# Two-layer GELU network on one core: w1's first four tiles as two transfers behind the identity, and two dummy matmuls fewer

## The chip, the cores and the metric

The kernel runs on one core of a Trainium2 chip. The metric is the device time of the launch in microseconds (us). The kernel before was run eight times: median 94.19 us, from 94.01 to 94.66.

## The reference

```python
B, S, D, F = 1, 2048, 448, 1792          # all inputs bf16
h = jnp.einsum("bsd,df->bsf", x, w1) + b1
h = jax.nn.gelu(h, approximate=True)
return jnp.einsum("bsf,fd->bsd", h, w2) + b2
```

## The kernel before, in words

The 2048 rows of x are taken in four chunks of 512 (`SC`). For each chunk, layer 1 computes the hidden values transposed: F = 14 tiles of 128, two tiles at a time in one PSUM unit (`Layer1`, pairs j = 0 to 6). The contraction over D = 448 is three slabs of 128 (`k` = 0 to 2) and one of 64 (`k` = 3). Every slab of 128 is cut in two halves of 64 rows, so that two matmuls stand side by side on the two row halves of the array. `a()` is the first half of such a pair, `b()` the second, which also has the slab of 64; `act()` then has ScalarE evict the unit as GELU(h + b1) into `g`. Layer 2 multiplies `g` by w2, VectorE adds b2 on eviction, and SP stores. All of this is written as lists of operations, one for each engine (`Program.op`, `Program.dma`), and `emit` puts each list out in its own order with the semaphore waits of each operation in front of it. An `after=` is such a wait. So the order on an engine is the order of the calls below.

The start is what the change touches. Chunk 0 of x is loaded untransposed (`xn`, line 153, first on SP's queue), and TensorE transposes it: four tiles t with three 128x128 transposes each (`turn`, line 338), and two more for the last 64 columns (line 359). Each needs the identity, which GpSimd makes (lines 167 and 168). VectorE evicts tiles 0 and 2, ScalarE tiles 1 and 3 (`evac`, line 345), and both evict the last columns (line 368). The other chunks come transposed by DMA (line 147).

Ahead of the transposes TensorE runs seven dummy matmuls of 512 columns on a constant (`warm(NWARM)`, line 191), then one of 256 (`warm(1, HC)`), and behind the transposes another one of 256. Their result isn't used.

w1's first 384 rows are loaded in three transfers cut at tiles 0, 4, 8, 14 (`W1CUTS`, `load_w1`, line 130). The first, w1(0) with tiles 0 to 3, is on ScalarE's queue behind the activation that loads the GELU table (line 175); the others are on SP's queue, in this order behind a wait for that activation: w1r(0), w1(1), w1r(1), w1(2), w2 in two transfers, b2, and the transposed x. w1r is w1's last 64 rows (line 137). VectorE copies parts of it to the other row half (line 382), in its list behind four 32x32 transposes and a cast of b1 (lines 180 and 182). b1 itself comes by GpSimd's queue (line 173).

The matmuls of chunk 0 begin with pair 0 and pair 1 on the first 256 columns (12 matmuls; these need x's tiles 0 and 1 and w1's tiles 0 to 3), then both on the other 256 columns, then pair 0's second half with w1r, then pair 2's first half, which needs w1(1):

```python
for h in (0, HC):
    L[0].a(h, h + HC)
    L[1].a(h, h + HC)
L[0].b()
L[2].a()
L[1].b()
```

All layer-1 and layer-2 matmuls are recorded at line 216.

Of the kernel before, what the change touches and what calls it, by code (L numbers as in the profile page):

```python
# [73 lines left out]
def bass_standalone__dense_activation_gelu__prompt_kernel(  # L74
# [10 lines left out]
    P = 128  # L85
    H = P // 2
    SC = 512
    HC = SC // 2
# [5 lines left out]
    D3 = KT * P  # L94
# [3 lines left out]
    with ExitStack() as es:  # L98
# [3 lines left out]
        ident = sb("ident", [P, P], BF16)  # L102
        xT = sb("xT", [P, KT + 1, S], BF16)
        w1_sb = sb("w1_sb", [P, KT, F], BF16)
# [15 lines left out]
        ones_m = one.broadcast_to([P, SC])  # L120


        W1CUTS = (0, 4, 8, 14)

        def w1_of(ft):
            return max(i for i, c in enumerate(W1CUTS) if c <= ft)

        def load_w1(i, engine="sync"):
            c0, c1 = W1CUTS[i] * P, W1CUTS[i + 1] * P
            pr.dma(engine, lambda e: e.dma_start(  # L130
                w1_sb[:, :, c0:c1], w1[0:D3, c0:c1].rearrange("(k p) f -> p k f", p=P)), ("w1", i))

        RCUTS = (0, 4, 14)

        def load_w1r(i, engine="sync"):
            cs = slice(RCUTS[i] * P, RCUTS[i + 1] * P)
            pr.dma(engine, lambda e: e.dma_start(w1r[H:P, cs], w1[D3:D, cs]), ("w1r", i))

        def load_w2(a, b):
            pr.dma("sync", lambda e: e.dma_start(  # L140
                w2_sb[:, a:b, :], w2[a * P:b * P, :].rearrange("(f p) d -> p f d", p=P)), ("w2", a))
# [11 lines left out]
        pr.dma("sync", lambda e: e.dma_start(xn[:, :, :], x0v), "x")  # L153
        pr.barrier("sync", ["table"])
        load_w1r(0)
        load_w1(1)
        load_w1r(1)
        load_w1(2)
        load_w2(0, 7)
        load_w2(7, 14)  # L160
        pr.dma("sync", lambda e: e.dma_start(b2_bc[:, :], b2.partition_broadcast(P)), "b2")
        for c in range(1, NSC):
            for slot in range(KT + 1):
# [9 lines left out]
        pr.dma("gpsimd", lambda e: e.dma_start(b1n[0:NFT, :], b1.rearrange("(c p) -> c p", p=P)), "b1n",  # L173
               after=["b1z"])
        pr.op("scalar", lambda e: e.activation(junk[:, :], one, ACT.Gelu_apprx_tanh), event="table")  # L175
        load_w1(0, "scalar")

        def turn_b1():
            for q in range(4):
                pr.op("vector", lambda e, q=q: e.transpose(  # L180
                    b1t[32 * q:32 * q + 32, :], b1n[:, 32 * q:32 * q + 32]), after=["b1n"], event=("b1t", q))
            pr.op("vector", lambda e: e.tensor_copy(b1_f[:, :], b1t[:, 0:NFT]),
                  after=[("b1t", q) for q in range(4)], event="b1")
# [5 lines left out]
        def warm(n, cols=SC):  # L189
            for _ in range(n):  # L190
                pr.op("tensor", lambda e: e.matmul(unit[0][:, 0, 0:cols], lhsT=ones_w, rhs=ones_m[:, 0:cols],  # L191
                                                   start=True, stop=True))
# [156 lines left out]
        def turn_all():  # L349


            pr.op("vector", lambda e: e.tensor_copy(  # L352
                xr[:, :, :].rearrange("p q (two h) -> p q two h", two=2),
                xn[:, :, D3:D].rearrange("p (q two) h -> p q two h", two=2)), after=["x"], event="xr_in")
            for t in range(STC):
                turn(t)
                evac(("vector", "scalar")[t % 2], t)
            for q in range(STC // 2):
                pr.op("tensor", lambda e, q=q: e.transpose(  # L359
                    stage(0)[:, q * P:(q + 1) * P], xr[:, q, :], ident[:, :]),  # L360
                    after=["xr_in", ("xT0", 0)], event=("xr", q))
            halves = (slice(0, H), slice(H, P))
            for src, engine in enumerate(("vector", "scalar")):
                i = stage(0)[halves[src], 0:2 * P].rearrange("p (q s) -> p q s", q=2)
                for dst in (src, 1 - src):
                    o = xT[halves[dst], KT, 0:SC].rearrange("p (q two s) -> p q two s", q=2, two=2)[:, :, src, :]
                    pr.op(engine, lambda e, o=o, i=i, engine=engine:
                          e.copy(o, i) if engine == "scalar" else e.tensor_copy(o, i),  # L368
                          after=[("xr", 0), ("xr", 1)], event=("xR0", dst, src))
            busy[(3, 0)] = ("xR0", 1, 0)  # L370
            busy[(3, 2)] = ("xR0", 0, 1)

        warm(NWARM)
        warm(1, HC)
        turn_all()
        warm(1, HC)
        turn_b1()

        for i in (0, 1):
# [3 lines left out]
                  after=[("w1r", i)], event=("w1rU", i))  # L383
# [12 lines left out]
        for c in range(NSC):  # L396
# [7 lines left out]
            else:  # L404

                pr.op("vector", lambda e: e.tensor_copy(b2_z[H:H + 1, :], b2_bc[H:H + 1, :]),  # L406
                      after=["b2", "b2z0"], event="b2z")
# [3 lines left out]
            p = Layer2(c, (0, 1))  # L411
# [46 lines left out]
```

## Time and profile before

| | us |
|---|---|
| median of 8 runs (lowest, highest) | 94.19 (94.01, 94.66) |
| the profiled execution | 94.12 |
| its span, first to last instruction | 92.8 |
| TensorE matmul busy | 89.8 (97% of the span) |
| ScalarE busy | 38.5 |
| VectorE busy | 13.4 |
| GpSimd busy | 1.7 |

The span is 1.3 us shorter than the time of the same execution. Engines in the views are PE (TensorE matmuls), PEld (its weight loads), DVE (VectorE), ACT (ScalarE), POOL (GpSimd) and SP; a q behind the name is the engine's instruction queue, where DMAs are issued. In the timeline the columns are start, duration, engine, line, operation, output<-input, shape, count, and in brackets how long the engine had been idle and who ended that. In the list of DMAs the last columns are the number of transfers, the size of each and the median time from issue to landing.

### The profile page before, as it was taken

The numbers are of one execution on the slowest core, as the hardware profiler recorded it, in microseconds if no ns is written. First come the engines' busy times: TensorE is split into PE (matmuls) and PEld (weight loads), VectorE is DVE, ScalarE is ACT, GpSimd is POOL, SyncE is SP. The second block draws the span as 40 slices with busy tenths as digits, with TensorE's granted clock in tenths as the row PEclk, the third lists the DMA queues.
The fourth block names the chain that finished last, engine by engine and source line by source line (L and its number), as shares of the span: only waits on it lengthen the run. The fifth ranks groups of instructions, "written<-read, shape, count | busy, mean of one in ns | idle before, by whom it ended". The sixth has DMA issues, their size and how long they took to land.

```text
span 92.8 us, 2060 instructions
## 1 busy us (share of the span) xinstructions
PE 89.8 (97%) x932; PEld 63.1 (68%) x932; DVE 13.4 (14%) x33; ACT 38.5 (41%) x63; POOL 1.7 (2%) x8
## 2 busy tenths in 40 slices
PE   6999999999999999999999999999999999999990
PEld 2486777666667777666667777666667777687990
DVE  0183001010432000000433000000233000000421
ACT  6065888700004787800003787900002888900001
POOL 6000000000000000000000000000000000000000
PEclk9999999999999999999999999999999999999999
DMA  2999999554657100000032000000022000000022
GB/s 37 365 270 320 373 301 143 107 112 87 70 104 203 32 0 7 0 0 0 0 106 99 0 0 4 0 7 0 0 99 99 7 0 0 0 0 7 27 72 99
DMA packets 12344, 7.32 MB, mean 79 GB/s; under 512 B 6960, under 2 KB 12144, under 8 KB 12336
## 3 DMA queue, kind: packets, MB, share of 16 engines
q1 hardware_dynamic: 11904, 6.80, 31.5%
q10 hardware_dynamic: 400, 0.39, 1.2%
q8 instruction: 7, 0.11, 0.5%
q0 software_dynamic: 32, 0.00, 0.0%
q14 instruction: 1, 0.01, 0.0%
HBM read 3.79 MB, written 1.84 MB: 61 GB/s over the span
## 4 chain that ended last, share of the span: by engine, by line
PE 97%; ACT 0%; issue 0%
PE u L216 92%; PE u L191 4%; PE u L338 1%; ACT out_sb L328 0%; PE u L359 0%
## 5 line engine op out<-in xcount | busy, mean ns | idle before, releaser
L268 ACT ACTIVATE g<-u,b_f 128x512 bf16<-128x512 f32 x56 | 35.0, 685 | 39.8 <-PE u L216 39.8
L216 PE MATMUL u<-w_sb,g 64*128 64x448 bf16 (+1 forms) x504 | 43.7, 328 | 0.0
L216 PE MATMUL u<-xT,w_sb 64*128 64x512 bf16 (+1 forms) x348 | 42.7, 369 | 0.0
L216 PEld LDWEIGHTS u<-w_sb,g 64*128 64x128 bf16 x504 | 30.8, 94 | 12.1
L216 PEld LDWEIGHTS u<-xT,w_sb 64*128 64x128 bf16 x348 | 26.8, 94 | 10.1 <-issue 0.2
L311 DVE TENSOR_TENSOR out_sb<-u,b_bc 128x448 bf16<-128x448 f32 x14 | 8.1, 620 | 59.8 <-PE u L216 59.8
L216 PE MATMUL u<-xT,w1r 64*128 64x512 bf16 x56 | 14.9, 376 | 0.0
L216 PEld LDWEIGHTS u<-xT,w1r 64*128 64x128 bf16 x56 | 5.3, 94 | 2.1 <-DVE w1r L382 0.3
L191 PE MATMUL u<-const-bfloat16-1.0 128*128 128x512 bf16 (+1 forms) x9 | 3.6, 562 | 0.8 <-PEq L443 0.8
L328 ACT CAST out_sb<-u 128x224 bf16<-128x224 f32 x1 | 0.3, 347 | 9.3 <-PE u L216 9.3
L191 PEld LDWEIGHTS u<-const-bfloat16-1.0 128*128 128x128 bf16 x9 | 1.1, 132 | 2.4 <-issue 2.4
L345 ACT COPY xT<-u 128x384 bf16<-128x384 bf16 x2 | 0.9, 480 | 2.7 <-PE u L338 2.7
L175 ACT ACT_TABLE_LOAD x1 | 1.3, 1283 | 0.7 <-PEq L443 0.7
L338 PEld LDWEIGHTS u<-ident,xn 128*128 128x128 bf16 x12 | 1.1, 128 | 0.6 <-issue 0.6
L186 DVE COPY xT<-xT 64x512 bf16<-64x512 bf16 x3 | 0.9, 289 | 3.7 <-DMA xT<-in_x_dram 3.6
L406 DVE COPY b_z<-b_bc 1x448 bf16<-1x448 bf16 x1 | 0.3, 269 | 6.7 <-DMA b_bc<-in_b_dram 6.7
L338 PE MATMUL u<-ident,xn 128*128 128x128 bf16 x12 | 1.2, 274 | 0.0
L319 DVE TENSOR_TENSOR out_sb<-u,b_bc 128x448 bf16<-128x448 f32 x1 | 0.6, 625 | 1.8 <-PE u L216 1.8
L180 DVE STREAM_TRANSPOSE b1t<-b1n 32x32 bf16<-32x32 bf16 x4 | 0.8, 202 | 0.1
L345 DVE COPY xT<-u 128x384 bf16<-128x384 bf16 x2 | 0.7, 358 | 0.6 <-PE u L338 0.6
L368 ACT COPY xT<-u 64x256 bf16<-64x256 bf16 x2 | 0.7, 368 | 0.0
L352 DVE COPY xr<-xn 128x256 bf16<-128x256 bf16 x1 | 0.2, 227 | 3.0 <-DMA xn<-in_x_dram 3.0
(18 smaller groups left out, 4.8 us busy)
## 6 DMA issues: line engine op xcount, KB each, us to landing
out_dram<-out_sb SPq DMA_DIRECT2D x16, 112.0 KB, 1.7
w_sb<-in_w_dram SPq DMA_DIRECT2D x2, 784.0 KB, 8.6
w_sb<-in_w_dram SPq DMA_DIRECT2D x1, 576.0 KB, 6.3
xn<-in_x_dram SPq DMA_DIRECT2D x1, 448.0 KB, 3.2
w_sb<-in_w_dram ACTq DMA_DIRECT2D x1, 384.0 KB, 4.2
w_sb<-in_w_dram SPq DMA_DIRECT2D x1, 384.0 KB, 4.4
xT<-in_x_dram SPq DMA_TRANSPOSE x12, 4.3
w1r<-in_w_dram SPq DMA_DIRECT2D x1, 160.0 KB, 4.3
```

What stands on the lines that cost most here:

```text
L175: pr.op("scalar", lambda e: e.activation(junk[:, :], one, ACT.Gelu_apprx_tanh), event="table")
L180: pr.op("vector", lambda e, q=q: e.transpose(b1t[32 * q:32 * q + 32, :], b1n[:, 32 * q:32 * q + 32]), after=["b1n"], event=("b1t", q))
L186: pr.op("vector", lambda e: e.tensor_copy(xT[0:H, KT, s0:s1], xT[H:P, KT, s0:s1]), after=after, event=event)
L191: pr.op("tensor", lambda e: e.matmul(unit[0][:, 0, 0:cols], lhsT=ones_w, rhs=ones_m[:, 0:cols], start=True, stop=True))
L216: o = pr.op("tensor", lambda e: e.matmul(unit[u][:, lo, cols], lhsT=lhsT, rhs=rhs, start=start, stop=stop, skip_group_check=skip), after=a ...
L268: pr.op("scalar", lambda e, lo=lo, ft=ft: e.activation(g[:, ft, c * SC:(c + 1) * SC], unit[u][:, lo, :], ACT.Gelu_apprx_tanh, bias=b1_f[:, ...
L311: pr.op("vector", lambda e, lo=lo, j=j: e.tensor_tensor(out=out_sb[:, j, :], in0=unit[u][:, lo, 0:D], in1=b2_bc[:, :], op=ALU.add), after= ...
L319: pr.op("vector", lambda e: e.tensor_tensor(out=out_sb[:, j, :].rearrange("p (two h) -> p two h", two=2), in0=unit[u][:, :, 0:DH], in1=b2_ ...
L328: pr.op("scalar", lambda e: e.copy(out_sb[:, j, DH:D], unit[u][:, 1, 0:DH]), after=[y[1]], event=("o", j, 1))
L338: pr.op("tensor", lambda e, k=k: e.transpose(stage(t)[:, k * P:(k + 1) * P], xn[:, t, k * P:(k + 1) * P], ident[:, :]), after=["ident", "x ...
L345: pr.op(engine, lambda e: e.copy(o, i) if engine == "scalar" else e.tensor_copy(o, i), after=[("xt", t)], event=("xT0", t))
L368: e.copy(o, i) if engine == "scalar" else e.tensor_copy(o, i),
```

## The change

It cuts w1's first transfer in two, tiles 0 and 1 and tiles 2 and 3, both on ScalarE's queue, the first of them behind a wait for the identity. What was w1(1) and w1(2) on SP's queue is now w1(2) and w1(3), with the same tiles. The 256-column dummy ahead of the transposes and the one behind them are gone; the seven of 512 columns stay.

```diff
-        W1CUTS = (0, 4, 8, 14)
+        W1CUTS = (0, 2, 4, 8, 14)
...
-        def load_w1(i, engine="sync"):
+        def load_w1(i, engine="sync", after=()):
             c0, c1 = W1CUTS[i] * P, W1CUTS[i + 1] * P
             pr.dma(engine, lambda e: e.dma_start(
-                w1_sb[:, :, c0:c1], w1[0:D3, c0:c1].rearrange("(k p) f -> p k f", p=P)), ("w1", i))
+                w1_sb[:, :, c0:c1], w1[0:D3, c0:c1].rearrange("(k p) f -> p k f", p=P)), ("w1", i), after)
...
         load_w1r(0)
-        load_w1(1)
+        load_w1(2)
         load_w1r(1)
-        load_w1(2)
+        load_w1(3)
...
-        load_w1(0, "scalar")
+
+        load_w1(0, "scalar", ["ident"])
+        load_w1(1, "scalar")
...
         warm(NWARM)
-        warm(1, HC)
         turn_all()
-        warm(1, HC)
         turn_b1()
```

## The prediction

> **What bounds the kernel now.** I read the page's chain first, then the chain in order of time, then the start in the timeline, then the DMA list with its times to landing. Chain in order of time (start, length, what):
>
> ```profile
> 0.78 3.36 PE u L191 x8
> 4.14 1.14 PE u L338 x12
> 5.28 0.11 PE u L359 x2
> 5.39 0.11 PE u L191
> 5.50 0.04 issue
> 5.53 85.11 PE u L216 x906
> 90.64 0.02 issue
> 90.66 0.35 ACT out_sb L328
> ```
>
> From 5.53 us on TensorE works 85 us without a hole. The change touches none of that work; it can only move the moment when it starts, or open a hole in its first microseconds. So the question is what makes 5.53. The chain names the dummy of line 191, but that is only the instruction before. The timeline of the start:
>
> ```profile
> 0.74 0.39 SPq L153 DMA_DIRECT2D xn<-in_x_dram  x1
> 0.80 0.43 ACTq L130 DMA_DIRECT2D w_sb<-in_w_dram  x1
> 1.18 0.29 POOL L168 TENSOR_SCALAR_AFFINE_SELECT ident<-ident 128x128 bf16<-128x128 bf16 x1 [0.23 <-POOL ident L167]
> 2.27 0.55 SPq L137 DMA_DIRECT2D w1r<-in_w_dram  x1
> 2.87 0.57 SPq L130 DMA_DIRECT2D w_sb<-in_w_dram  x1
> 3.96 0.23 DVE L352 COPY xr<-xn 128x256 bf16<-128x256 bf16 x1 [3.04 <-DMA xn<-in_x_dram]
> 4.04 1.06 PEld L338 LDWEIGHTS u<-ident,xn 128*128 128x128 bf16 x12 [0.60 <-issue]
> 4.91 0.88 ACT L345 COPY xT<-u 128x384 bf16<-128x384 bf16 x2 [2.67 <-PE u L338]
> 5.22 0.27 PE L191 MATMUL u<-const-bfloat16-1.0 128*128 128x256 bf16 x1
> 5.50 0.14 PEld L216 LDWEIGHTS u<-xT,w_sb 64*128 64x128 bf16 x4 [0.23 <-issue]
> 7.37 0.22 DVE L382 COPY w1r<-w1r 64x256 bf16<-64x256 bf16 x1
> ```
>
> and of the DMA list:
>
> ```profile
> xn<-in_x_dram SPq DMA_DIRECT2D x1, 448.0 KB, 3.2
> w_sb<-in_w_dram ACTq DMA_DIRECT2D x1, 384.0 KB, 4.2
> w_sb<-in_w_dram SPq DMA_DIRECT2D x1, 384.0 KB, 4.4
> w1r<-in_w_dram SPq DMA_DIRECT2D x1, 64.0 KB, 3.4
> ```
>
> x lands at 0.74 + 3.2 = 3.94, and 0.1 later the transposes start (4.04). ScalarE evicts tile 1 from 4.91 on, 0.48 each, so to 5.39; 0.11 later the first real weight load stands at 5.50. w1(0) had landed at 0.80 + 4.2 = 5.0. So the start is x, transposes, ScalarE's eviction; w1(0) has some 0.4 us in hand.
>
> **First dummy.** The seven of 512 columns take 0.43 us each (their weight loads stand 0.43 apart), so they are issued out at 0.78 + 7 x 0.42 = 3.72. The eighth, half as wide, runs to about 3.94. That is just where x lands. Without it nothing starts sooner as long as x lands at 3.94: gain 0. It is worth something only if x comes sooner, up to 0.2 us; then it would have been the limit.
>
> **Second dummy.** It begins at 5.22 and holds the array for half of what a wide one takes: 0.21 us at the slow clock of the dummies, about 0.11 at the full one. In this execution it is done at 5.33 and the eviction releases the matmuls at 5.50: gain 0, cover 0.17. But the clock matters. The row of the transposes' weight loads reads
>
> ```profile
> L338 PEld LDWEIGHTS u<-ident,xn x12: 97/147/147, 4.0 to 5.0; 128*128 128x128 bf16 x12
> ```
>
> 147 ns at first and 97 at the last: the array runs slowly (dummies 0.43 apart; the page's clock row, full from the start, doesn't show this) and becomes fast at about 4.9. If it becomes fast later, the 14 transposes at 0.107 (9 start in the slow stretch 4.04 to 4.95) end their issue at 4.08 + 1.50 = 5.58 and the dummy at 5.79: then it holds up the matmuls by 0.21. The eight runs spread over 0.65 us, which the moment of the switch would explain (a microsecond of real matmuls at half clock costs 0.5). I take half the runs at 0.2: gain 0.1 in the median, bounds 0 and 0.21.
>
> **Transposes and the clock.** Here the Trainium skill speaks against the change ("TensorE: Matmul & The Clock Gate", Part 4: PE-mode transpose): in transpose mode the activity monitor doesn't count TensorE as busy, so the full clock doesn't engage. By that rule the two dummies are the only counted work between 3.7 and 5.5, and taking them away could cost a further window of slow clock, by Part 1 of that page 3.4 us, so half of it, 1.7 us. The row says otherwise: the clock rose inside the transposes, 0.9 us after the last dummy of the first group. And if uncounted transposes decided it, some of the eight runs should lie 1.7 us higher; the highest is 0.54 above the profiled one. I take 0 for this, with 1.7 as the bound at a small chance.
>
> **w1(0) issued later.** Today the issue starts at 0.80, 0.06 after x's, and x's first data competes with it at best in its set-up. In windows of the start the DMA engines move 172 GB/s from 2.0 to 2.5 us and 409 from 2.5 to 3.0. The slow first half microsecond costs x about 0.5 x (1 - 172/409) = 0.29 us. Whether ScalarE's transfer is the cause no view can say. If all of it goes, x lands 0.29 sooner; if none, 0; if the two new issues (1.5 and 1.95) disturb x midway, x could be 0.1 later. I take 0.1 sooner: the DMAs are different queues with one set of engines, and only part of the slow start need be theirs. With the first dummy gone, transposes, evictions and VectorE's chain (to line 382, which ends at 7.59 and for which a weight load waits today, 0.3 us in the waits) all follow x: the gain of 0.1 is not swallowed there.
>
> **The added wait.** The identity is done at 1.18 + 0.29 = 1.47. ScalarE's wait holds up nothing: its activation for the table is already in the engine (2.03), and its next work is at 4.91. Two issues of 0.43 end at 2.4. SP's queue waits for the activation, not for these.
>
> **When the two halves land.** w1(0), 393 KB, landed 1.1 us behind x. At that rate each half takes 0.55 us: 4.5 and 5.05. In the trace's packet records (not printed in a view) a packet of 256 bytes takes 18 ns, one of 1,024 bytes 46. The rows shrink from 1,024 to 512 bytes, by interpolation 27 ns, 48 rows for each DMA engine instead of 24: 1.30 us instead of 1.10, so 0.2 us more of DMA time (bounds 0 and 1.1, where a row costs the same at any length). First half 4.6, second 5.25. Needed: 5.4 for the first; for the second 5.53 + 6 matmuls of 0.055 = 5.86. Both are covered.
>
> **Who comes between.** SP's w1r(0) is issued at 2.27 and the next w1 at 2.87, against 1.95 for the second half. The Trainium skill ("DMA: Bandwidth & Descriptors", Queues, rings and completion order) says that each DMA engine takes turns between queues, a whole packet of descriptors at a time. By turns, the second half waits for w1r(0), 64 KB or 0.2 us, and lands at 5.45; if it had to let SP's 384 KB by as well, at 6.5, which is 0.65 late. The rows: a store of 112 KB needs 1.7 us to landing on idle queues, but w1r(0), 64 KB, took 3.4 and landed at 5.6, behind w1(0) at 5.0. So a transfer begun is drained first, and the order is about that of the issues. I take the first.
>
> **What the 0.2 us of DMA time does further on.** SP's next w1 lands at 2.87 + 4.4 = 7.3; pair 2 loads its first weights at 7.66. At 7.5 plus the 0.1 of a release it is just in time: cost 0, cover 0.06; if that is gone, up to 0.2. The last w1 transfer (10.3, needed at 10.7) stands alike.
>
> **Sum.** Profiled execution: 94.12 (span 92.8 and 1.3 around it) - 0.1 (x) - 0 (dummies, in its own clock phase) = 94.0. The median of the runs is 0.07 above it, and there the second dummy gives 0.1 more: 94.19 - 0.1 - 0.1 = 94.0.
>
> **The rivals.** *x gets the whole slow start back.* For it: 172 against 409 GB/s, and a first dummy that would have hidden just this. Against it: the rate may be low at the start of any load. 0.29 + 0.1: 93.8, down to 93.6. *Nothing moves.* x lands as before and the second dummy is covered: 94.15 to 94.25. *The second half, or SP's next w1, comes too late* (slower). Mechanism: ScalarE's second transfer falls behind SP's 384 KB; the price is (6.5 + 0.1) - 5.86 = 0.7 at pair 1's first matmul, less 0.2 of gain: 94.7. It decides from a landing of the second half later than 5.75, or of SP's w1 later than 7.55. For it: only 0.3 and 0.06 us in hand, and x itself took 1.0 us from issue to the first data (none move before 1.75). Against it: the issue is 0.9 us ahead of SP's. *The clock rises a window later* (slower): 95 to 95.7 in the runs that it hits.
>
> **How the numbers follow.** Small gain, 94.0 (93.75 to 94.25): 0.44. Large gain, 93.75: 0.17. Nothing: 0.10. Late weights, 94.7: 0.22. Clock: 0.07. A measurement of this kernel can tell about 0.3% (0.28 us). Faster by that (under 93.91): the large gain and under half of the small one, 0.35. Slower (over 94.47): most of late weights and clock, 0.27. Within: 0.38. The range from 93.6 to 94.7 leaves out the clock and half of late weights. The likeliest case alone: 93.75 to 94.25.
>
> **What would show it.** Right: x's copy on VectorE (line 352) at about 3.86 instead of 3.96, line 345 and the first weight load of line 216 sooner by as much, no wait of line 216 for a DMA, and weight loads of 97 ns by 5.5. Wrong: a wait on a w_sb transfer at 5.9 or 7.7 (late weights); weight loads of 147 ns behind 6 us (clock); line 352 at 3.96 (nothing gained at x).

## The result, and the profile after

The changed kernel takes 95.77 us (median of 11 runs, 94.86 to 97.75) against 94.28 (32 runs, 93.88 to 94.82): ratio 1.0123, interval 1.0093 to 1.0153. So it is slower, by about 1.2%; the prediction was 94.0, with a range up to 94.7. The ratio leaves out four executions of 97.2 to 97.8 us, in which the mean granted clock was 0.982 instead of 1.000; the median of 95.77 holds them, and without them it is 95.53.

The profiled execution took 95.26 us with a span of 93.9, 1.1 more than before. The chain in order of time (start, length, what):

```profile
0.74 1.18 ACT L175
1.92 0.03 issue
1.95 5.03 DMA w_sb<-in_w_dram
6.97 0.05 issue
7.02 84.75 PE u L218 x903
91.77 0.38 DVE out_sb L327
```

The chain no longer leads to TensorE's first matmuls but to a transfer of w1: issued at 1.95, that is ScalarE's second one, and landed at 6.97, 5.03 us later (line 218 is line 216 of before, moved by two). The timeline of the start shows the hole that it leaves:

```profile
1.50 0.96 ACTq L130 DMA_DIRECT2D w_sb<-in_w_dram  x2
2.87 0.57 SPq L130 DMA_DIRECT2D w_sb<-in_w_dram  x1
4.08 0.23 DVE L354 COPY xr<-xn 128x256 bf16<-128x256 bf16 x1 [3.15 <-DMA xn<-in_x_dram]
5.59 0.50 PE L218 MATMUL u<-xT,w_sb 64*128 64x256 bf16 x6
7.01 1.31 PEld L218 LDWEIGHTS u<-xT,w_sb 64*128 64x128 bf16 x24 [1.20 <-DMA w_sb<-in_w_dram]
7.02 1.80 PE L218 MATMUL u<-xT,w_sb 64*128 64x256 bf16 x24 [0.93 <-DMA w_sb<-in_w_dram]
```

Pair 0's six matmuls run at 5.59, on the first half of the weights, 0.06 later than before. The seventh matmul stood at 5.86 before and stands at 7.02 now. From there to the end of the matmuls both kernels take the same: 90.64 - 5.86 = 84.78 before, 84.75 after. So the 1.16 us by which the seventh matmul came later (0.06 of them from pair 0's later start, the rest from the wait) are the whole difference of the spans. x brought nothing: VectorE's copy, which shows x's landing, is at 4.08, not at the hoped 3.86. And while the second half was under way the DMA engines moved little (last column, GB/s; ahead of it the share of the time in which they were busy):

```profile
4.00:4.50 0.50, 0.31 (x4) 0.34 (x5) 0.23 (x1) 0.00 (x0) 0.00 (x0) 1.00 0.69 178
4.50:5.00 0.50, 0.50 (x10) 0.50 (x9) 0.29 (x1) 0.04 (x1) 0.00 (x0) 1.00 0.72 136
5.00:5.50 0.50, 0.48 (x7) 0.21 (x4) 0.42 (x2) 0.50 (x2) 0.00 (x0) 1.00 0.98 222
```

The kernel before in the same three windows:

```profile
4.00:4.50 0.50, 0.50 (x6) 0.46 (x6) 0.19 (x1) 0.00 (x0) 0.00 (x0) 1.00 1.10 374
4.50:5.00 0.50, 0.50 (x8) 0.50 (x6) 0.36 (x1) 0.09 (x1) 0.00 (x0) 1.00 0.89 201
5.00:5.50 0.50, 0.50 (x8) 0.27 (x5) 0.35 (x1) 0.50 (x2) 0.00 (x0) 1.00 0.94 317
```

It has such a dip too, but only when the data of its first w1 transfer are already through (its last packet ends at 4.53).

The packet records of the traces (printed in no view) show more of the late half. Each of these loads ends with sixteen packets of four bytes, apparently one for each of the 16 DMA engines. For w1(0) before, they lie between 4.28 and 4.52; for the second half after, between 4.48 and 6.60, eight of them by 5.54. So the landing tells of the last engine, and half of them were through a microsecond earlier. From 4.0 to 5.0 us ScalarE's queue has 227 packets of weights and SP's only 37, with the engines busy 0.7 of the time: SP's data aren't what slows the half in this microsecond. From 5.0 on, ScalarE's last 163 packets of 512 bytes stand among SP's, which are 311 of 1,024 bytes by 6.5.

### The profile page after: what moved, and what is told of

The parts are those of the page before. It is cut to its first block, busy times and chain, and to the rows that moved or that the text cites. A ratio compares the mean times of both kernels' runs of the same rounds, so it can differ in the third digit from the quotient of the medians.

```text
span 93.9 us, 2057 instructions
## 1 busy us (share of the span) xinstructions
PE 89.6 (95%) x930; PEld 46.0 (49%) x930; DVE 13.4 (14%) x33; ACT 38.4 (41%) x63; POOL 1.7 (2%) x8
## 4 chain that ended last, share of the span: by engine, by line
PE 90%; DMA 5%; ACT 1%; DVE 0%; issue 0%
PE u L218 90%; DMA w_sb<-in_w_dram 5%; ACT L175 1%; DVE out_sb L327 0%
## 5 line engine op out<-in xcount | busy, mean ns | idle before, releaser
L218 PE MATMUL u<-w_sb,g 64*128 64x448 bf16 (+1 forms) x504 | 43.2, 328 | 0.0
L218 PE MATMUL u<-xT,w_sb 64*128 64x512 bf16 (+1 forms) x348 | 41.0, 369 | 1.0 <-DMA w_sb<-in_w_dram 0.9
L218 PEld LDWEIGHTS u<-w_sb,g 64*128 64x128 bf16 x504 | 24.5, 94 | 18.4
L218 PEld LDWEIGHTS u<-xT,w_sb 64*128 64x128 bf16 x348 | 16.8, 94 | 20.4 <-DMA w_sb<-in_w_dram 1.2
L218 PE MATMUL u<-xT,w1r 64*128 64x512 bf16 x56 | 10.6, 376 | 0.0
L218 PEld LDWEIGHTS u<-xT,w1r 64*128 64x128 bf16 x56 | 2.7, 94 | 3.3
L193 PE MATMUL u<-const-bfloat16-1.0 128*128 128x512 bf16 x7 | 3.1, 624 | 0.8 <-PEq L443 0.8
L382 DVE COPY w1r<-w1r 64x256 bf16<-64x256 bf16 (+1 forms) x2 | 0.6, 288 | 1.4 <-DMA w1r<-in_w_dram 1.4
```

The costliest lines, as they stand in the source:

```text
L218: o = pr.op("tensor", lambda e: e.matmul(unit[u][:, lo, cols], lhsT=lhsT, rhs=rhs, start=start, stop=stop, skip_group_check=skip), after=a ...
L382: pr.op("vector", lambda e, odd=odd: e.tensor_copy(odd(slice(0, H)), odd(slice(H, P))), after=[("w1r", i)], event=("w1rU", i))
```

## The experiments

Theory after the result: the second half is late because it is issued 0.7 us later and so meets the transfers of SP's queue at the DMA engines (sharing). Rivals: the shorter rows and the further transfer are slow by themselves; the dummies' absence costs the time through the clock. Landings below are each from one profiled execution. How far they vary is seen in three kernels with the same loads (the changed kernel, `e2_w1_only` and `e7_filled_wait`): 6.97, 7.43 and 6.54. So a difference of less than 0.9 us between two single landings says little.

**Each part alone.** `e1_dummies_only`: the kernel before with this edit only.

```diff
         warm(NWARM)
-        warm(1, HC)
         turn_all()
-        warm(1, HC)
         turn_b1()
```

> The kernel before without its two 256-column dummies, w1 loaded as before. If the late second transfer is the whole cost (theory: sharing of the DMA engines), this run has no wait for w1 and takes 94.1 to 94.3, like before. If the dummies' absence costs the time through the clock (rival), it takes 95 or more, or some of its executions lie about 1.7 us higher with a mean granted clock near 0.98.

Ratio 1.0006, 0.9989 to 1.0022. The dummies' removal costs nothing and gains nothing that can be measured; the mean granted clock is 1.000 in all 22 executions.

`e2_w1_only`: the changed kernel with the two `warm(1, HC)` put back.

> The changed kernel with the two dummies put back: only the w1 loads are changed. Sharing theory: the wait at pair 1's first matmul stays, the second transfer lands near 7.0, 95.3 to 95.8. Clock rival: close to before, 94.2 to 94.5.

Ratio 1.0178, 1.0136 to 1.0221, mean clock 1.000 in all six executions; the second half lands at 7.43, 0.46 later than in the changed kernel's profile. The median, 96.04, is above the expected range; the interval of the ratio overlaps that of the changed kernel. The whole loss is in the w1 loads.

**The wait or the split.** `e3_no_wait`:

```diff
-        load_w1(0, "scalar", ["ident"])
+        load_w1(0, "scalar")
```

> The changed kernel without the wait for the identity: two transfers, issued from 0.8 on. Sharing theory: the second half is issued at about 1.25, data 0.7 us ahead of where it is in the changed kernel, begun before SP's w1 (issued at 2.87) has data; it lands by about 5.3 and no wait opens: 94.1 to 94.4. Rival (shorter rows and one more transfer are what is slow): the second half still lands after 6 and the time stays over 94.9.

The halves are issued at 0.80 and 1.26 and land 3.8 and 4.3 us later; no wait opens at pair 1. Median 94.60, above the expected range; ratio 1.0023, 1.0006 to 1.0041. The landing of the second half, 5.54, is 0.2 later than expected and 0.5 later than the one transfer of before (5.05); in the packet records its data end at 4.71 against 4.53. That is the split's own price as far as two single executions can tell, and it is hidden here up to 5.86. A part of what remains is one transfer later on: SP's last w1 lands at 10.97 instead of 10.36, and its first user waits 0.5 us.

`e4_one_transfer`: the delay without the split.

```diff
-        W1CUTS = (0, 2, 4, 8, 14)
+        W1CUTS = (0, 4, 8, 14)
...
         load_w1(0, "scalar", ["ident"])
-        load_w1(1, "scalar")
```

> The changed kernel with one transfer of four tiles on ScalarE's queue, behind the identity: the delay without the split. Sharing theory: the one transfer begins when x ends, as the first half does now (landing 4.6), but its second half's worth of rows meets SP's w1r(0) and w1 and shares with them: it lands between 5.3 and 6, and all 24 first matmuls wait for it: 94.4 to 95.0. Rival (rows and the number of transfers): it lands at 5.1 as before, 94.2.

Median 94.87, ratio 1.0050, 1.0025 to 1.0074. Issued 0.7 us later, the one transfer lands at 6.16, 1.1 later than before. So the delay alone costs time, without shorter rows and without a second transfer; that the landing moves by more than the delay is within the spread of single landings here. For the two halves it moves further: the second is issued 0.7 us later than in `e3_no_wait` and lands at 6.54 to 7.43 instead of 5.54. In time, the split alone costs 0.2%, the delay alone 0.5%, and both together 1.2%.

**Who is beside it.** `e5_sp_held`:

```diff
         load_w1r(0)
-        load_w1(2)
+        load_w1(2, after=[("w1", 1)])
```

> The changed kernel with SP's next w1 transfer (384 KB) and all behind it on SP's queue held until w1's second half has landed; only w1r(0), 64 KB, still runs beside it. Sharing theory: the second half lands by about 5.3 and pair 1 doesn't wait; SP's w1 is issued at 5.4 instead of 2.87 and lands near 8.0, so a wait of about 0.3 us opens at pair 2: 94.3 to 94.8. Rival (a transfer issued from 1.95 on ScalarE's queue is late by itself, by its issue or its short rows): the second half lands near 7.0 as before, and SP's w1 later still: over 96.

The second half lands at 5.94, a microsecond sooner than in the changed kernel, but not at 5.3. The second expectation failed clearly: SP's w1, issued at 5.96 on idle engines, landed 4.06 us later, at 10.02, and pair 2 waited 2.5 us instead of 0.3. Ratio 1.0224, 1.0176 to 1.0271; what it measures is mainly this second wait. It rests on two executions: in the other four, the profiled one among them, the mean clock was 0.982. In the profile the clock falls at 10.4 us, behind both landings.

`e6_one_queue`: both halves on SP's queue, ahead of w1r(0), just as late.

```diff
         pr.dma("sync", lambda e: e.dma_start(xn[:, :, :], x0v), "x")
+        load_w1(0, after=["ident"])
+        load_w1(1)
         pr.barrier("sync", ["table"])
...
-        load_w1(0, "scalar", ["ident"])
-        load_w1(1, "scalar")
```

> The changed kernel with both halves of w1's first four tiles on SP's queue, behind x and the same wait for the identity, ahead of w1r(0): issued at 1.5 and 2.05, as late as in the changed kernel, but in one queue with what follows. Sharing theory (turns are taken between queues, and one queue keeps its order): the halves land near 4.6 and 5.2, no wait at pair 1; SP's w1 is issued 0.35 later but its data queue anyway: 94.1 to 94.4. Rival (late issue or short rows): the second half lands after 6.5, 95 to 96.

The first half lands at 4.58, as expected, the second at 6.34, not 5.2: between the two theories, nearer to the second. Median 94.98, ratio 1.0052, 1.0026 to 1.0078. One queue in place of two isn't the cure, so turns between queues are at most a part.

`e7_filled_wait`: eight dummies in the wait.

```diff
             L[0].a(h, h + HC)
+            if h == 0:
+                for _ in range(8):
+                    pr.op("tensor", lambda e: e.matmul(unit[1][:, 0, 0:HC], lhsT=ones_w, rhs=ones_m[:, 0:HC],
+                                                       start=True, stop=True))
             L[1].a(h, h + HC)
```

> The changed kernel with eight 256-column dummies (on a PSUM unit that is cleared afterwards) between pair 0's first six matmuls and pair 1's, that is, inside the wait for w1's second half. If the wait alone is the cost, the dummies (0.86 us at full clock) lie within it: 95.0 to 95.8, as the changed kernel. If standing still for a microsecond also costs clock, the mean granted clock is 1.000 in all executions and the median falls below the changed kernel's 95.77.

Ratio 1.0150, 1.0104 to 1.0196. The second half came at 6.54 here and pair 1 began at 6.69, when the dummies were through. The mean clock is 1.000 in all six executions, but the median, 95.76, didn't fall: inconclusive for the time.

**Rows.** `e9_by_slab`: the first four tiles as one transfer of 128 rows and one of 256, all of 1,024 bytes.

```diff
-        load_w1(0, "scalar", ["ident"])
-        load_w1(1, "scalar")
+        for k0, k1, after in ((0, 1, ["ident"]), (1, KT, [])):
+            pr.dma("scalar", lambda e, k0=k0, k1=k1: e.dma_start(
+                w1_sb[:, k0:k1, 0:SC], w1[k0 * P:k1 * P, 0:SC].rearrange("(k p) f -> p k f", p=P)), ("w1k", k0), after)
```

> The changed kernel with the first four tiles cut by slabs of the contraction instead of by tiles: one transfer of 128 rows of 1,024 bytes and one of 256, behind the identity, both on ScalarE's queue; the number of rows and their length are those of the one transfer. Theory that the number of rows is the price (each row costs DMA time whatever its length, once the engines have used up what was queued): the last of the two lands as in the run with one delayed transfer, 5.5 to 6.2, and the time is 94.6 to 95.0. Theory that being a second transfer on ScalarE's queue beside SP's is the price: it lands near 7, 95.3 or more.

The last of the two lands at 6.41, 0.2 outside the first theory's window; median 95.10, ratio 1.0078, 1.0052 to 1.0104. It lies between the theories again. Half as many rows save about a third of the change's loss, with intervals that overlap; landings with a spread like the one above can't split it further.

`e10_probes`: the kernel before with loads into unused tiles in the middle of the kernel, each step behind the landing of the one before.

```diff
+                probe("sync", mz[0][:, :, :], cut(3, 256, 0), "pa", ["outA"])
+                probe("scalar", mz[1][:, :, :], cut(3, 256, 256), "pb", ["outA"])
+                probe("sync", mz[2][:, :, :], cut(3, 256, 0), "pc", ["pa", "pb"])
+                probe("sync", mz[3][:, :, :], cut(3, 256, 256), "pd", [])
+                probe("sync", mz[4][:, :, :], cut(3, 256, 512), "pe", ["pc", "pd"])
+                probe("sync", mw[:, :, :], cut(3, 512, 0), "pf", ["pe"])
+                probe("sync", ml[:, :], w2[0:D3, :].rearrange("(p t) d -> p (t d)", t=3), "pg", ["pf"])
+                probe("sync", ms[:, :], w1[0:P, 0:256], "ph", ["pg"])
```

> The kernel before with loads into unused tiles while the DMA engines are idle (behind chunk 0's stores); the outputs don't use them. First 384 rows of 512 bytes on SP's and on ScalarE's queue at once; then two such on SP's queue; then alone: 384 rows of 512, 384 rows of 1,024, 128 rows of 2,688, 128 rows of 512 bytes. If the number of rows is the price, 384 rows of 512 and of 1,024 bytes take nearly the same, about 3 to 4 us from issue to landing, and 128 long rows (344 KB) under 3. If turns between queues are the price, the pair on two queues takes over 1 us longer than the pair on one queue. If bytes are (what the prediction took), 384 rows of 512 bytes are 0.5 us quicker than those of 1,024, and both pairs are alike.

From its list of DMAs (size, us from issue to landing; ma and mb are the pair on two queues, mc and md the pair on one, the others alone):

```profile
mw_<-in_w_dram SPq DMA_DIRECT2D x1, 384.0 KB, 3.3
ml_<-in_w_dram SPq DMA_DIRECT2D x1, 336.0 KB, 2.9
ma_<-in_w_dram SPq DMA_DIRECT2D x1, 192.0 KB, 3.2
mb_<-in_w_dram ACTq DMA_DIRECT2D x1, 192.0 KB, 3.5
mc_<-in_w_dram SPq DMA_DIRECT2D x1, 192.0 KB, 2.7
md_<-in_w_dram SPq DMA_DIRECT2D x1, 192.0 KB, 2.8
me_<-in_w_dram SPq DMA_DIRECT2D x1, 192.0 KB, 3.1
ms_<-in_w_dram SPq DMA_DIRECT2D x1, 64.0 KB, 1.8
```

Alone, 384 rows of 512 bytes take 3.1 us and of 1,024 bytes 3.3: half the bytes save next to nothing. But a second such transfer right behind the first adds only 0.6 (the pair on one queue is issued at 33.78 and 34.21 and ends at 37.0), as the prediction's 27 ns a row has it (24 rows for each engine, 0.65). The pair on two queues ends 3.5 us after its issue, against 3.2 on one: turns cost 0.25 at most, and two transfers as alike as mc and me differ by 0.4. None of the three explanations gives 1.5 us by itself where nothing else is under way.

**How much company.** `e11_b1_on_sp` moves b1's transfer from GpSimd's queue to SP's, behind w1r(0).

> The changed kernel with b1's transfer (3.5 KB) moved from GpSimd's queue to SP's, behind w1r(0). If b1's packets from a third queue cause the slow stretch from 4.0 to 5.0 us, the second half lands by about 5.3 and the time is 94.2 to 94.5. If it is SP's w1 beside it, the second half still lands near 7, 95.3 to 95.8.

The second half lands at 6.85, so b1's queue isn't what makes it late. The median, 95.06, lies between the two expectations (ratio 1.0082, 1.0055 to 1.0108): about a third of the loss is gone, with intervals that overlap. If that is real, its cause isn't shown, since the move also puts SP's next w1 later (issued at 3.50 instead of 2.87). In this profile the first half was late, too: it landed at 5.76, and pair 0 waited 0.6 us for it. With the loads of the changed kernel it landed at 4.64, 4.55 and 5.03, so the prediction's cover for it (needed at 5.4) wasn't safe, either.

`e13_sp_one_ahead`:

```diff
         load_w1(2)
+        pr.barrier("sync", [("w1", 1)])
         load_w1r(1)
```

> The changed kernel with SP's w1r(0) and next w1 issued as now, but everything behind them on SP's queue held until w1's second half has landed. If SP's next w1 alone is the company that matters, the second half still lands at 6.5 to 7. If the further issues are (their descriptors), it lands near 5.9, as with all of SP held. Later transfers come late in both cases, so the time is over 95 and says little.

It lands at 6.69 (94.98 us, one execution), within the spread of the kernels with all of SP's transfers beside it: SP's next w1 is company enough.

`e14_alone`: the wait of SP's queue is for the second half, too, and b1 is on SP's queue behind w1r(0).

```diff
-        pr.barrier("sync", ["table"])
+        pr.barrier("sync", ["table", ("w1", 1)])
         load_w1r(0)
```

> The changed kernel with the two halves alone behind x: SP's queue, w1r(0) too, is held until the second half has landed, and b1 is on SP's queue behind that. If company is the cause, the halves land at 4.6 and 5.2, as the prediction worked out. If the start itself is slow (any second transfer behind x), the second half lands near 5.9 again. The time is over 96 in both cases, since all later weights are late.

The tile view of w_sb, for ScalarE's two transfers alone:

```profile
L130 ACTq DMA_DIRECT2D w_sb<-in_w_dram x2: 415/464/512, 1.5 to 1.9; - x2
DMA to landing us min/median/max: 3.4/3.5/3.5
```

They land at 4.90 and 5.45, and pair 1 waits for nothing. That is the 5.25 of the prediction within 0.2. (97.16 us, since all later weights come late.) In the packet records ScalarE's queue has 406 packets of weights from 4.0 to 5.0 us, instead of the changed kernel's 227, and the second half's four-byte packets lie between 4.50 and 5.16.

In the order of company the second half lands at 5.45 (none), 5.94 (w1r(0) and b1), 6.69 (SP's next w1 as well), 6.97 (all). Each is one execution; the first two lie clear of the 6.54 to 7.43 in full company, the third doesn't. The pieces of the chains (start, length) from which the landings of `e4_one_transfer`, `e5_sp_held`, `e6_one_queue` and `e13_sp_one_ahead` are read, in this order:

```profile
1.50 4.66 DMA w_sb<-in_w_dram
1.95 4.00 DMA w_sb<-in_w_dram
1.93 4.41 DMA w_sb<-in_w_dram
1.94 4.75 DMA w_sb<-in_w_dram
```

**A faster kernel?** `e8_w1r_first` is the kernel before without the two dummies and with VectorE's first copy of w1r ahead of b1's transposes:

```diff
-        turn_b1()
...
                   after=[("w1r", i)], event=("w1rU", i))
+            if i == 0:
+                turn_b1()
```

> An attempt at a faster kernel: the kernel before without the two dummies, with VectorE's first copy of w1r (line 382) ahead of b1's transposes and cast. In the profiles a weight load waits 0.3 to 0.4 us for that copy. The copy would end at about 6.35 instead of 7.6, b1 at 7.6, still ahead of the first GELU (7.9). One row half of the array gets its stall of 0.15 us back: 94.1 to 94.2 if it counts in full, 94.3 if the other row half sets the end.

Median 94.15 against 94.44 of the kernel before beside it, ratio 0.9983, 0.9963 to 1.0003: probably a little faster, not told apart from no change. `e12_w1r_first_b1_sp` is the same with b1 on SP's queue:

> The attempt at a faster kernel (kernel before without the two dummies, w1r's copy ahead of b1's transposes) with b1 on SP's queue behind w1r(0). If b1's queue causes the slow stretch, the other w1 transfers land sooner and nothing waits: 94.0. If not, as without the move, 94.15; b1 may land later than 5.3, but is needed only at 6.4.

Median 94.49, above both expectations; ratio 1.0021, 1.0005 to 1.0037: the move takes that away again. Here, too, SP's next w1 is issued at 3.50 instead of 2.87, and weight loads wait for w1 0.9 us in all.

## Why the prediction was wrong

- **Who comes between.** This is the step that failed. It took from w1r(0) and w1(0) that "a transfer begun is drained first, and the order is about that of the issues", and put the second half at 5.45. It landed at 6.97; without company at 5.45 (`e14_alone`), where the prediction had 5.25, so that the same figure twice is chance. Taking away SP's later transfers, SP's next w1, and w1r(0) with b1's queue gives back 0.3, 0.75 and 0.5, in one execution each. A single transfer issued 0.7 later lost 1.1 (`e4_one_transfer`). The row that I read as a rule showed a transfer 1.5 us ahead of the others, and the second half is 0.3 ahead of w1r(0) and 0.9 of SP's w1.
- **The rule that I set aside.** The Trainium skill ("DMA: Bandwidth & Descriptors", Queues, rings and completion order) has the engines take turns between queues. As the bound the prediction let SP's 384 KB by and got 6.5. That was nearer than my choice, and still short: the turns are at most 0.25 us where measured alone (`e10_probes`), and one queue for all brought 0.6 of 1.5 (`e6_one_queue`). What remains goes with the low rate between 4.0 and 5.5 us, 136 to 222 GB/s, in whose first microsecond SP's queue hardly moved data. The prediction worked with about 360 throughout (393 KB in 1.1 us) and made nothing of the window of 201 that the kernel before has at 4.5.
- **The slower rival.** Its place (pair 1's first matmul), its deciding point (5.75) and its mechanism (ScalarE's second transfer behind SP's 384 KB) were right but for one point: SP's 384 KB didn't go first. They landed at 8.4, and the two transfers went side by side. Its price was mis-sized: 0.7 less 0.2 of gain; measured 1.16 and no gain. Its chance, 0.22, came from the failed step.
- **x sooner.** Wrong. x takes 3.1 to 3.3 us to landing in every kernel here, with w1 issued at 0.8 or at 1.5, and the rate from 2.0 to 2.5 is no higher after the change (129 GB/s against 172). In the packet records SP's queue is the only one with data until 3.1 us, in the kernel before, too: no data of w1 stand beside x's slow start. What makes it slow stays open.
- **Dummies.** 0 for the first, as said; the 0.1 for the second isn't seen (1.0006, 0.9989 to 1.0022; 0.1 us would be the lower edge). By the Trainium skill ("TensorE: Matmul & The Clock Gate", Part 4: PE-mode transpose) TensorE doesn't count as busy in transpose mode and the full clock doesn't engage; the prediction set the 1.7 us that this could cost at nothing. That held: no execution of `e1_dummies_only` took more than 94.70 us, and in its profile the weight loads of the transposes take 95 to 98 ns, as at the full clock. Whether the transposes helped to raise it isn't shown, since the seven wide dummies stayed. The mean clock of 1.000 doesn't show it, because the kernel before has that mean, too, with a rise as late as 4.9.
- **The clock a window later.** No execution of the kernel before or of `e1_dummies_only` had it, but four of the changed kernel's twelve (with the profiled one) did. In the profiles of two such executions (`e11_b1_on_sp`, `e5_sp_held`) the granted clock is 0.50 for 3.4 us, from 6.9 and from 10.4, right behind waits for w1 of 0.6 and of 2.1 us. Half of 3.4 is 1.7; the four executions lie 1.7 to 2.2 above the 95.53 of the others. The prediction looked for this in the transposes, and not behind a hole.
- **The added wait** holds up nothing on ScalarE, as said, but the price of a later issue was reckoned only by the engine's own work, not by who is next at the DMA engines.
- **The 0.2 us of DMA time.** Where nothing else was late the data of the two halves did end 0.18 later than those of one transfer (`e3_no_wait`). The cost further on wasn't seen behind the hole, since all of pair 2 came 1.2 later. In `e3_no_wait`, where nothing hides it, SP's last w1 was 0.6 late.

**Open:** why company slows the DMA engines to half their rate there, when a pair in mid-kernel hardly shows it; and why some executions had the lower clock and others of the same kernel not. It was seen only in kernels in which TensorE waits for w1 without dummies at hand: in 12 of 74 executions (four of six in `e5_sp_held`, none of ten in `e6_one_queue`), and in none of the 12 with dummies (`e2_w1_only`, `e7_filled_wait`). These are too few to show it.

## What to carry to other kernels

The first loads of a kernel are a queue in time: a transfer that is needed first must be issued first, with more lead than its bytes call for, and moving its issue by 0.7 us behind a convenient event may cost over a microsecond once the next queue's transfers catch up with it. Ask of a delayed load not who waits on its engine but whose transfers it will now meet. A landing that looks protected in the profile may only have been early: measure it in company before relying on it. And a landing is that of the last DMA engine: the mean rate doesn't give it.

## What the runs showed of the hardware

In one execution each, a load of 384 rows takes 3.1 us from issue to landing on idle queues with rows of 512 bytes and 3.3 with 1,024; 128 rows of 512 bytes take 1.8. So halving the bytes of such a transfer hardly makes it land sooner. At the start of the kernel the loads of 384 rows of 512 bytes are slower: 3.4 to 3.5 us for the two alone behind x, and 4.6 to 5.5 for the second of them with all of SP's transfers beside it. By the four-byte packets the DMA engines end their parts of that second transfer 2.1 us apart in the changed kernel (4.48 to 6.60), and those of w1(0), which ran ahead of the others, 0.24 us apart in the kernel before (4.28 to 4.52). In the profile of `e11_b1_on_sp` the granted clock fell to half for 3.4 us behind two waits of TensorE of 0.6 us; the mean clock of the other twelve executions of that kernel is 1.000.
